# Half tiles of h, split k^T v and a new order of steps in a fused attention and gated convolution kernel

## Chip, cores and metric

The kernel runs on one core of one Trainium2 chip. The metric is the device time of one execution in microseconds; it is quoted as the median of several runs. The core has five engines that run their own instruction queues in order and wait for each other through semaphores: TensorE (PE in the profile, its weight loads PEld), VectorE (DVE), ScalarE (ACT), GpSimd (POOL) and SyncE (SP). PE writes only to PSUM, which has eight banks of 512 fp32 columns; DVE and ACT read it there.

## What is computed

Linear attention without softmax, a normalisation over each head, and a feed-forward layer with a convolution as its gate (8 batches, 8 heads, 576 tokens, head size 64, model 512, inner size 1024):

```python
kv  = einsum('bhsd,bhse->bhde', k, v)
o   = einsum('bhsd,bhde->bhse', q, kv)
x   = o / sqrt(mean(o*o, -1) + 1e-6) * g_norm      # heads side by side: (8, 576, 512)
h   = maximum(x @ w_in, 0)                          # (8, 576, 1024)
c   = conv_w[0]*h[s-1] + conv_w[1]*h[s] + conv_w[2]*h[s+1]
out = (h * sigmoid(c)) @ w_out                      # (8, 576, 512)
```

Inputs and output are fp32; the kernel multiplies in bf16 and accumulates in fp32.

## The kernel before

The order of all work is written out by hand as one long string, `ORDER`. Each word names a step, its arguments and, after `@`, the slots that it takes: a PSUM bank (0 to 7), or a place in a ring of SBUF buffers. The kernel calls the steps in this order, and at the end it ties each engine's instructions to exactly this sequence. So an engine never overtakes a step of its own that waits; what a step waits for follows from the buffers that it reads and takes over.

The steps that matter here, for batch `b`, pair of head tiles `u` (two pairs, `u` = 0, 1), token half `s` (two halves of 288 tokens; batch 0 has 256 and 320) and block `f` of 128 of the 1024 inner columns:

- `pre`, `af`, `ps`, `pl`, `pn`, `pc`, `dg`: the first loads, the identity matrix and small constants. `ps` is twelve small DVE instructions, `pl` nine.
- `cad`, `caa`: casts of batch 0's staged q, k, v to bf16 on DVE or ACT. The other batches are loaded and cast by POOL's DMAs: `Lq`, `Lk`, `Lv`; `Li` loads half of w_in, `Lo` w_out. POOL's queue issues them in their order.
- `qt`, then `qd` or `qa`: q transposed on PE into a bank, copied out by DVE or ACT. `kv.b.u0.n`: k^T v for `n` pairs; `kva`, `kvd`: its copy.
- `ot`: o for one pair and token half. `sq`: its square on ACT. `on` or `oq`: the sum over a head, by a matmul with ones. `nl`: the reciprocal root on ACT. `mo`: x out of o on DVE.
- For batches 4 to 7 the sums of two batches share one bank: `oc` (copy of o), `ss`, `ln`, `sl`, `sp`, `mu` take the place of `on`, `nl`, `mo`.
- `hm.b.f`: one h tile, 8 matmuls of 288 columns into two banks, four for each token half. `re.b.f`: its ReLU on ACT, 576 columns at once. Batch 0 uses `hp` and `rp`, one token half in one bank.
- `ta`, `aa`, `ab` on DVE, `sg` on ACT and `mg` on DVE: taps, sum, sigmoid and gate; `cv`, `sc` do this for four blocks of batch 0 on PE and ACT.
- `om.p.m.f0.n`: half of an output tile of 128 tokens of the batch pair `p`; `ea`, `ed`: its copy by ACT or DVE; `st`: its store by SP. The last tile is `oh`, `eh` or `dh`, `sh`.
- `fi.n.512`: n filler matmuls of zeros, whose result is not used.

In the profile the lines are: L266 `fi`, L382 `kv`, L394 and L396 its copy, L413 `qt`, L440 `ot`, L448 `sq`, L461 and L470 the sums, L478 `nl`, L489 `mo`, L546 `hm`, L552 `re`, L561 `hp`, L568 `rp`, L611 `cv`, L635 `om`, L641 and L646 its copies, L341 `Li`, L327 the loads of q, k, v, L310 and L311 `ps`, L215 ACT's table loads. The reciprocal root and the sigmoid lie in different table sets; the load is issued where the order goes from one to the other.

Of the kernel before, what the change touches and what calls it, by code (L numbers as in the profile page):

```python
# [61 lines left out]
caa.q.1.0 ot.0.0.0@6 sq.0.0.0@0 fi.2.512@1 caa.v.3.0 qt.0.1.0@2 qa.0.1.0@1 oq.0.0.0@4 nl.0.0.0@0 fi.1.512@1 fi.3.512@0  # L62
mo.0.0.0@0 Lk.1.0.4@1 Lv.1.0.4@1 kv.0.1.1@2 fi.1.512@0 Li.4.4 qt.0.0.1@4 Lo.0.8 Lq.2.0.4@2 qd.0.0.1 Lk.2.0.4@0
Lv.2.0.4@0 kva.0.1.1 ot.0.1.0@0 fi.3.512@2 sq.0.1.0@1 oq.0.1.0@6 nl.0.1.0@1 cad.q.1.1 qt.0.1.1@4 qd.0.1.1 ot.0.0.1@2
ot.0.1.1@4 sq.0.0.1@2 sq.0.1.1@3 fi.1.512@6 mo.0.1.0 oq.0.0.1@6 nl.0.0.1@2 fi.1.512@0 fi.1.512@0 mo.0.0.1 oq.0.1.1@0
fi.1.512@6 nl.0.1.1@3 hp.0.0@6 hp.3.0@7 hp.2.0@0 rp.2.0@0 hp.1.0@1 mo.0.1.1 hp.3.1@2 rp.0.0 rp.3.0 pc dg.3 dg.1
hp.1.1@0 rp.1.1 rp.3.1 hp.0.1@3 rp.0.1 dg.0 dg.2 rp.1.0 hp.2.1@4 rp.2.1 qt.1.0.0@6 qd.1.0.0@2 qt.1.1.0@2 qd.1.1.0@3
cv.0.1@0 sc.0.1@0 cv.0.0@4 sc.0.0 mg.0.1.0 cv.0.3@6 sc.0.3@1 cv.0.2@2 sc.0.2 mg.0.1.1 kv.1.0.2@0 kva.1.0.2@1
ot.1.0.1@4 sq.1.0.1@4 ot.1.1.0@6 oq.1.0.1@2 nl.1.0.1@4 mo.1.0.1@1 hp.7.1@0 rp.7.1 hp.6.1@1 rp.6.1 sq.1.1.0@5 hp.7.0@2
rp.7.0 ta.0.1.7@0 Lq.3.0.4@0 Lk.3.0.4@1 Lv.3.0.4@1 Lq.4.0.4@1 hp.6.0@0 rp.6.0 ta.0.1.6 hp.5.0@1 rp.5.0 on.1.1.0@4  # L70
nl.1.1.0@5 mo.1.1.0 ot.1.1.1@2 sq.1.1.1@6 hp.5.1@0 rp.5.1 ta.0.1.5@1 aa.0.1.3 ab.0.1.3 hp.4.1@1 rp.4.1 oq.1.1.1@4
ot.1.0.0@6 nl.1.1.1@6 mo.1.1.1 sq.1.0.0@7 hp.4.0@0 rp.4.0 om.0.0.0.4@1 on.1.0.0@4 nl.1.0.0@7 mo.1.0.0 om.0.3.0.4@0
qt.2.0.0@4 qd.2.0.0@4 qt.2.1.0@2 sg.0.1.7 hm.1.7@6 re.1.7 sg.0.1.6 hm.1.0@4 re.1.0 ta.0.1.4 aa.0.1.2 qd.2.1.0@0
hm.1.1@6 re.1.1 ab.0.1.2 mg.0.1.3 hm.1.2@2 sg.0.1.4 sg.0.1.5 re.1.2 hm.1.3@4 re.1.3 hm.1.4@6 re.1.4 ta.1.1.0@0
ta.1.1.1 aa.1.1.0 ab.1.1.0 sg.1.1.0 sg.1.1.1 kv.2.0.2@2 kvd.2.0.2@2 mg.0.1.2 om.0.1.0.4@4 qt.3.1.0@6 ot.2.0.1@2
sq.2.0.1@0 qd.3.1.0@1 om.0.0.4.4 ed.0.0@0 om.0.3.4.4 ed.0.3@1 ta.1.1.3@1 on.2.0.1@6 om.0.1.4.4 nl.2.0.1@8 mo.2.0.1@2
ed.0.1@2 ot.2.1.1@0 sq.2.1.1@1 ot.2.1.0@6 sq.2.1.0@2 om.0.2.0.4@5 on.2.1.1@2 nl.2.1.1@9 mo.2.1.1 om.0.2.4.4 ea.0.2@3
kv.3.0.2@2 kva.3.0.2@0 on.2.1.0@4 nl.2.1.0@0 mg.1.1.0 mo.2.1.0 ot.2.0.0@0 sq.2.0.0@3 hm.1.6@2 re.1.6 on.2.0.0@4
ta.1.1.2 nl.2.0.0@1 mo.2.0.0 ot.3.1.1@6 sq.3.1.1@4 hm.1.5@2 re.1.5 qt.3.0.0@4 on.3.1.1@0 nl.3.1.1@2 hm.2.5@2 re.2.5@1
# [47 lines left out]
def kernel(  # L127
# [84 lines left out]
    def act_table(which):  # L212
        if act_set[0] != which:
            act_set[0] = which
            nc.scalar.preload_act_table_set(  # L215
                {"rs": "abs_reciprocal_sqrt_and_small", "sig": "sigmoid_and_others"}[which])
# [511 lines left out]
```

## Time and profile before

| | us |
|---|---|
| median of 3 runs | 182.23 (182.22 to 182.25) |
| the profiled execution | 182.22 |
| its span, first to last instruction | 180.1 |
| PE busy | 169.2 |
| ACT busy | 148.8 |
| DVE busy | 148.4 |
| POOL busy | 20.5 |

The span and the busy times come from one profiled execution. The time of an execution is 2.1 us longer than its span. Matmuls are pipelined, so the duration of one in the profile (286 ns for 288 columns) is longer than the distance between two that follow each other; for ACT and DVE too the durations of neighbours overlap a little. The rows that the prediction uses are shown there.

### The profile page before, as it was taken

To read this page: it belongs to the slowest core of one execution; us is meant where nothing else is said; L and a number is where in the kernel's file an instruction comes from. 1 tells how busy PE (TensorE), PEld (TensorE's weight loads), DVE (VectorE), ACT (ScalarE), POOL (GpSimd) and SP (SyncE) were. 2 spreads that over 40 slices of the span, in tenths; PEclk is the share of its full clock that TensorE was granted. 3 is DMA by queue.
4 is the path that set the end of the run, shared out by engine and by line. 5 is a ranking of instruction groups with operands and counts; after the bars stand their busy time and mean duration, and the time that the engine had idled before them with its cause. 6 is when DMAs were issued, how large, how long until landed. Compare 5 with 4: busy or idle time off the path is not lost. (4 is left out here: it accounts for less than half of the span.)

```text
span 180.1 us, 5305 instructions
## 1 busy us (share of the span) xinstructions
PE 169.2 (94%) x2243; PEld 101.5 (56%) x2259; DVE 148.4 (82%) x286; ACT 148.8 (83%) x235; POOL 20.5 (11%) x32
## 2 busy tenths in 40 slices
PE   7878997999999999999999999999999999999991
PEld 2343765577456677546567764445578754444450
DVE  3496853999867899897999999989999899999730
ACT  2377798999888999999989999999699984738830
POOL 3195104000331121030000000000000000000000
PEclk9999999999999999999999999999999999999999
DMA  5999999999999999999440000401160000441495
GB/s 165 393 310 209 208 206 208 208 208 207 208 208 257 208 207 209 207 167 226 143 161 5 0 4 0 151 28 58 64 231 0 0 0 4 175 175 66 175 337 183
DMA packets 20807, 27.80 MB, mean 154 GB/s; under 512 B 1188, under 2 KB 15280, under 8 KB 20784
## 3 DMA queue, kind: packets, MB, share of 16 engines
q0 software_dynamic: 13248, 14.50, 47.7%
q1 hardware_dynamic: 6992, 11.80, 18.2%
q10 hardware_dynamic: 544, 1.18, 1.7%
q8 instruction: 17, 0.28, 0.6%
q14 instruction: 6, 0.05, 0.1%
HBM read 32.52 MB, written 9.44 MB: 233 GB/s over the span
## 5 line engine op out<-in xcount | busy, mean ns | idle before, releaser
L635 PE MATMUL banks<-w_out_sb,h 128*128 128x512 bf16 x267 | 62.8, 379 | 0.9 <-issue 0.5
L546 PE MATMUL banks<-x,w_in_sb 128*128 128x288 bf16 x448 | 58.2, 286 | 0.4 <-ACT rs L478 0.2
L546 PEld LDWEIGHTS <-w_in_sb 128*128 128x128 bf16 x448 | 42.9, 98 | 13.3 <-issue 1.0
L601 ACT ACTIVATE taps<-taps,cw 128x576 bf16<-128x576 bf16 (+1 forms) x44 | 40.6, 958 | 6.5 <-DVE taps L595 6.4
L635 PEld LDWEIGHTS <-h 128*128 128x128 bf16 x280 | 26.3, 98 | 30.5 <-issue 1.5
L552 ACT ACTIVATE h<-banks 128x576 bf16<-128x576 f32 x56 | 34.4, 666 | 2.8 <-PE banks L546 2.2
L625 DVE TENSOR_TENSOR h<-h,taps 128x1152 bf16<-128x1152 bf16 (+1 forms) x24 | 22.8, 953 | 3.6 <-ACT taps L601 1.6
L448 ACT ACTIVATE sq<-banks 128x576 bf16<-128x576 f32 (+2 forms) x32 | 20.9, 686 | 1.8 <-PE banks L440 1.8
L590 DVE TENSOR_TENSOR taps<-taps 128x1152 bf16<-128x1152 bf16 (+1 forms) x22 | 21.5, 977 | 0.5
L595 DVE TENSOR_TENSOR taps<-taps,h 128x1152 bf16<-128x1152 bf16 (+1 forms) x22 | 21.3, 973 | 0.4
L641 ACT ACTIVATE row<-banks 128x512 f32<-128x512 f32 x27 | 15.7, 617 | 4.8 <-PE banks L635 4.1
L584 DVE TENSOR_SCALAR taps<-h,cw 128x576 bf16<-128x576 bf16 (+1 forms) x44 | 18.4, 419 | 1.4 <-ACT h L568 0.7
L489 DVE SCALAR_TENSOR_TENSOR x<-banks,cw,rs 128x576 bf16<-128x576 f32 (+2 forms) x16 | 12.9, 814 | 6.9 <-ACT rs L478 6.8
L585 DVE TENSOR_SCALAR taps<-h,cw 128x576 bf16<-128x576 bf16 (+1 forms) x44 | 18.5, 420 | 0.0
L215 ACT ACT_TABLE_LOAD x10 | 12.8, 1283 | 1.9 <-issue 1.8
L423 DVE COPY qT<-banks 128x1152 bf16<-128x1152 bf16 (+2 forms) x17 | 11.8, 702 | 1.7 <-PE banks L413 1.4
L532 DVE SCALAR_TENSOR_TENSOR x<-o,cw,banks 128x576 bf16<-128x576 f32 x16 | 12.3, 809 | 1.1 <-PE banks L526 1.1
L478 ACT ACTIVATE rs<-banks,eps_sb 128x576 f32<-128x576 f32 (+2 forms) x16 | 11.8, 746 | 1.2 <-PE banks L470 0.5
L266 PE MATMUL banks<-zero 128*128 128x512 bf16 x35 | 10.4, 426 | 1.6 <-DVE zero L245 1.2
L454 ACT ACTIVATE o<-banks 128x576 f32<-128x576 f32 x16 | 10.5, 710 | 0.0
L440 PE MATMUL banks<-qT,kvb 64*64 64x288 bf16 (+2 forms) x128 | 8.5, 297 | 1.4 <-ACT kvb L396 0.9
L327 POOL DMA_DIRECT2D k_sb<-in_k_dram x7 | 5.3, 751 | 38.1 <-PE banks L382 28.2
(80 smaller groups left out, 127.0 us busy)
## 6 DMA issues: line engine op xcount, KB each, us to landing
out_dram<-row SPq DMA_DIRECT2D x35, 256.0 KB, 2.5
q_sb<-in_q_dram POOLq DMA_DIRECT2D x7, 576.0 KB, 16.3
k_sb<-in_k_dram POOLq DMA_DIRECT2D x7, 576.0 KB, 11.6
v_sb<-in_v_dram POOLq DMA_DIRECT2D x7, 576.0 KB, 14.2
stg<-in_v_dram ACTq DMA_DIRECT2D x2, 576.0 KB, 6.4
stg<-in_k_dram SPq DMA_DIRECT2D x4, 288.0 KB, 6.9
w_in_sb<-in_moe_w_in_dram POOLq DMA_DIRECT2D x2, 512.0 KB, 11.2
w_out_sb<-in_moe_w_out_dram POOLq DMA_DIRECT2D x1, 1024.0 KB, 19.4
```

The source lines that it names most:

```text
L448: nc.scalar.activation(T["sq", b, u, s], T["o", b, u, s], AX.Square)
L489: nc.vector.scalar_tensor_tensor(x_part(b, u, s), T["o", b, u, s], g_sb, T["rs", b, u, s], op0=AL.mult, op1=AL.mult)
L546: nc.tensor.matmul(ps[:, s, :c1 - c0], w_in_sb[:, t, f * P:(f + 1) * P], T["x", b][:, t, c0:c1], start=(t == 0), stop=(t == NT - 1))
L552: nc.scalar.activation(h_of(b, f), T["hm", b, f][:, :, :HS].rearrange("p e (r n) -> p e n r", r=R), AX.Relu)
L584: nc.vector.tensor_scalar_mul(tap[:, 0, f % 2, :n, 8:8 + S], h[:, f], cw[:, f:f + 1])
L585: nc.vector.tensor_scalar_mul(tap[:, 1, f % 2, :n, :S], h[:, f], cw[:, 2 * NF + f:2 * NF + f + 1])
L590: nc.vector.tensor_add(tap[:, 1, :, :n, :S], tap[:, 0, :, :n, 7:7 + S], tap[:, 1, :, :n, 1:1 + S])
L595: nc.vector.tensor_add(y, y, span(b, n)[:, 2 * j:2 * j + 2])
L601: nc.scalar.activation(y, y, AX.Sigmoid, scale=cw[:, NF + f:NF + f + 1])
L625: nc.vector.tensor_mul(h, h, tap_of(b, j)[:, 1, :, :n, :S])
L635: nc.tensor.matmul(T["om", p, m], h[:, f, m * P:(m + 1) * P], w_out_sb[:, f, :], start=(f == 0), stop=(f == NF - 1))
L641: nc.scalar.activation(T["os", p, m], T["om", p, m], AX.Copy)
```

## The change

1. The h tiles of batches 1 to 3 are made by token halves: `hs.b.f.s` makes 4 matmuls of 288 columns into one bank, `rh.b.f.s` does the ReLU of 288 columns. 24 `hm` and 24 `re` become 48 `hs` and 48 `rh`. Batches 4 to 7 keep `hm` and `re`.
2. `kv.1.0.2` becomes `kv.1.0.1` and `kv.1.1.1`, with a copy each (one on ACT, one on DVE).
3. POOL's queue gets the second half of w_in in front of q, k and v of batch 1; before it stood behind them.
4. The whole `ORDER` is new: other places for nearly all steps and banks, 44 filler matmuls where there were 38, eight output copies fewer or more on one or the other engine (ACT's 27 become 23, DVE's 8 become 12, and of the two short ones at the end DVE takes one). ACT runs 253 instructions where it ran 235, DVE 293 where it ran 286.

Steps that no word of `ORDER` calls (`tq`, `kz`, `kx`, `ox`, `sv`) are added too, and with them the names `TQ`, `GW` and `width`. As no word calls `tq`, `TQ` is empty, `GW` is `HS` as before, and all widths are as they were.

```diff
 ORDER = """
-pre@0,1 pl fi.10.512@0 af cad.q.0.0@0 caa.v.0.0@0 caa.k.0.0@0 qt.0.0.0@2 gt.k.1.0 cad.v.1.0 Li.0.4 Lq.1.0.4@1
-fi.13.512@0 qd.0.0.0@0 cad.k.1.0 ct@0 kv.0.0.1@4 kva.0.0.1@0 ps cad.v.2.0 pg cad.k.2.0 cad.k.3.0 cad.q.0.1 fi.1.512@1
...
-cv.0.1@0 sc.0.1@0 cv.0.0@4 sc.0.0 mg.0.1.0 cv.0.3@6 sc.0.3@1 cv.0.2@2 sc.0.2 mg.0.1.1 kv.1.0.2@0 kva.1.0.2@1
-ot.1.0.1@4 sq.1.0.1@4 ot.1.1.0@6 oq.1.0.1@2 nl.1.0.1@4 mo.1.0.1@1 hp.7.1@0 rp.7.1 hp.6.1@1 rp.6.1 sq.1.1.0@5 hp.7.0@2
...
-hm.1.1@6 re.1.1 ab.0.1.2 mg.0.1.3 hm.1.2@2 sg.0.1.4 sg.0.1.5 re.1.2 hm.1.3@4 re.1.3 hm.1.4@6 re.1.4 ta.1.1.0@0
...
+pre@0,1 fi.10.512@0 af ps gt.k.1.0 Li.0.4 cad.q.0.0@0 qt.0.0.0@2 caa.v.0.0@0 pn fi.8.512@0 ct@0 fi.5.512@1 cad.v.1.0
+pg cad.k.1.0@0 caa.k.0.0 kv.0.0.1@4 fi.2.512@0 kva.0.0.1@0 qd.0.0.0@0 ot.0.0.0@6 fi.2.512@0 cad.q.1.0 qt.0.1.0@2
...
+qt.0.1.1@2 qd.0.1.1 ot.0.0.1@0 sq.0.0.1@2 mo.0.1.0 ot.0.1.1@2 sq.0.1.1@3 fi.1.512@6 oq.0.0.1@6 nl.0.0.1@2 pl mo.0.0.1
+fi.1.512@4 oq.0.1.1@4 nl.0.1.1@3 mo.0.1.1 hp.2.0@6 hp.0.0@7 rp.0.0@0 hp.3.0@4 rp.2.0 pc dg.2 dg.0 dg.3 Li.4.4
+Lq.1.0.4@1 Lk.1.0.4@1 dg.1 hp.1.0@5 rp.1.0 hp.2.1@7 hp.0.1@6 rp.0.1 rp.3.0 hp.1.1@5 rp.1.1 hp.7.0@0 rp.7.0 rp.2.1
...
+ab.0.1.3 cv.0.3@6 sc.0.3@0 cv.0.2@2 sc.0.2 mg.0.1.1 hp.5.1@4 rp.5.1 kv.1.0.1@6 kva.1.0.1@1 hp.5.0@5 rp.5.0 ot.1.0.0@0
+sq.1.0.0@4 ot.1.0.1@2 kv.1.1.1@6 sq.1.0.1@5 kvd.1.1.1 ta.0.1.4@0 ta.0.1.5 aa.0.1.2 fi.1.512@4 fi.1.512@4 oq.1.0.0@4
+nl.1.0.0@4 mo.1.0.0@1 fi.6.512@6 oq.1.0.1@6 nl.1.0.1@5 mo.1.0.1 ot.1.1.1@4 sq.1.1.1@6 ot.1.1.0@6 sq.1.1.0@7 oq.1.1.1@0
+ab.0.1.2 nl.1.1.1@6 mo.1.1.1 om.0.0.0.4@2 on.1.1.0@0 nl.1.1.0@7 mo.1.1.0 om.0.1.0.4@3 hs.1.3.1@4 Lq.2.0.4@2 qt.2.1.0@0
+qd.2.1.0@4 qt.2.0.0@6 hs.1.0.1@5 qd.2.0.0@0 sg.0.1.5 sg.0.1.4 hs.1.1.1@0 rh.1.1.1 mg.0.1.2 hs.1.1.0@1 rh.1.1.0
...
+om.0.6.4.4 ed.0.6@0 ss.4.4.2@7 ss.5.4.2 ln.4@0 sl.4@0 qt.6.0.0@4 qd.6.0.0@1 qt.6.1.0@0 qa.6.1.0@4 hs.3.7.1@2 rh.3.7.1
+hs.3.4.0@3 rh.3.4.0 hs.3.6.1@7 rh.3.6.1 hs.2.4.1@6 st.0.8 rh.2.4.1 hs.3.6.0@0 rh.3.6.0 hs.3.5.1@1 rh.3.5.1
+sp.4.1.0.4@2 mu.4.1.0@1 sp.4.1.1.4@6 hs.2.7.1@0 rh.2.7.1 mu.4.1.1 hs.3.4.1@1 rh.3.4.1 sp.4.0.0.4@4 mu.4.0.0
+sp.4.0.1.4@2 mu.4.0.1 sg.2.2.3 hs.3.5.0@0 hs.3.7.0@1 rh.3.5.0 sp.5.1.0.4@6 mu.5.1.0@0 kv.6.0.2@4 kvd.6.0.2@0
+hs.2.6.0@2 rh.2.6.0 sp.5.0.1.4@6 mu.5.0.1 hm.4.5@4 sp.5.1.1.4@2 rh.3.7.0 sp.5.0.0.4@0 mu.5.0.0 mu.5.1.1 sg.2.2.0
...
 """
...
+    @op
+    def hs(b, f, s):
+        c0, c1 = cols(b, s)
+        ps = T["hs", b, f, s] = bank()[:, :c1 - c0]
+        for t in range(NT):
+            nc.tensor.matmul(
+                ps, w_in_sb[:, t, f * P:(f + 1) * P], T["x", b][:, t, c0:c1],
+                start=(t == 0), stop=(t == NT - 1))
+
+    @op
+    def rh(b, f, s):
+        ps, h = T["hs", b, f, s], h_of(b, f)
+        if b in TQ:
+            h, fr = h.rearrange("p (n r) -> p n r", r=R)[:, :, s::2], ps.rearrange("p (g n) -> p n g", n=PS)
+        else:
+            h = h[:, s * HS:(s + 1) * HS].rearrange("p (n r) -> p n r", r=R)
+            fr = ps.rearrange("p (r n) -> p n r", r=R)
+        nc.scalar.activation(h, fr, AX.Relu)
```

More of the change, by code (lines that the diff above doesn't have):

```diff
@@ L75 @@
[L75 to L79, printed above, removed]
@@ L123 @@
+ea.3.4@0 st.3.4 oh.3.8.0@3 dh.3.8.0@5 sh.3.8.0 oh.3.8.1@2 eh.3.8.1@4 sh.3.8.1
 """
@@ L216, in act_table @@
                 {"rs": "abs_reciprocal_sqrt_and_small", "sig": "sigmoid_and_others"}[which])
+    TQ = {int(tok.split("@")[0].split(".")[1]) for tok in ORDER.split() if tok.startswith("tq.")}
     RS = ((0, 4), (4, 9))
+    GW = 320 if TQ else HS
     HEAD = (("sync", "q.0.0 k.0.1 k.1.1 q.1.0 k.2.1 k.3.1 q.0.1 q.1.1"), ("scalar", "v.0.2 v.2.2"))
@@ L223, in cols, with width @@
             return tuple(r * D for r in RS[s])
+        if b in TQ:
+            return s * 5 * D, (5 + s * 4) * D
         return s * HS, (s + 1) * HS
+    def width(b, s):
+        c0, c1 = cols(b, s)
+        return c1 - c0
     @op
@@ L444, in sq, with tq, kz, kx @@
     @op
+    def tq(b, u):
+        T["qT", b, u] = ring("qT", [P, 2, S], BF16, "qT").rearrange("p a s -> p (a s)")
+        nc.sync.dma_start_transpose(
+            out=T["qT", b, u].rearrange("p (g c) -> p g c", c=P),
+            in_=qkv["q", b][:, 2 * u:2 * u + 2, :].rearrange("p t c -> p (t c)"))
+    @op
+    def kz(b, u0, n):
+        k_sb, v_sb = qkv["k", b], qkv["v", b]
+        ps = T["kv", b, u0] = bank2()
+        for u in range(u0, u0 + n):
+            for r in range(R):
+                for tt in range(2):
+                    for i in range(2):
+                        nc.tensor.matmul(
+                            ps[half(tt), i, u * D:(u + 1) * D],
+                            k_sb[half(i), 2 * u + tt, r * D:(r + 1) * D],
+                            v_sb[half(i), 2 * u + tt, r * D:(r + 1) * D],
+                            start=(r == 0), stop=(r == R - 1))
+    @op
+    def kx(b):
+        T["kvx", b] = ring("kvx", [P, 2, 2 * D], BF16, "kvx")
+        for i in range(2):
+            nc.sync.dma_start(out=T["kvx", b][half(i)], in_=T["kvb", b][half(1 - i)])
+    @op
+    def ox(b, u, s):
+        ps = T["o", b, u, s] = bank2()[:, :, :width(b, s)]
+        qt_sb = T["qT", b, u].rearrange("p (g i c) -> p g i c", i=2, c=D)
+        kv_sb = T["kvx" if s else "kvb", b]
+        for tt in range(2):
+            c = half(tt ^ s)
+            g0 = (tt * R + s) // 2
+            for i in range(2):
+                nc.tensor.matmul(
+                    ps[half(i), tt, :].rearrange("p (g c) -> p g c", c=D),
+                    kv_sb[c, i, u * D:(u + 1) * D], qt_sb[c, g0:g0 + 5 - s, i, :],
+                    start=True, stop=True)
+    @op
     def sq(b, u, s):
@@ L448, in sq, with sv @@
         nc.scalar.activation(T["sq", b, u, s], T["o", b, u, s], AX.Square)
+    @op
+    def sv(b, u, s):
+        c0, c1 = cols(b, s)
+        T["sq", b, u, s] = ring("sq", [P, 2, 320], BF16, "sq")[:, :, :c1 - c0]
+        nc.vector.tensor_mul(T["sq", b, u, s], T["o", b, u, s], T["o", b, u, s])
     @op
@@ L494, in ss @@
         if b == b0:
-            T["ss", b0] = bank()[:, :HS]
+            T["ss", b0] = bank()[:, :GW]
         for s in range(2):
@@ L504, in ln @@
     def ln(b0):
-        r = T["rs", b0] = ring("rs", [P, HS], FP32, "rs")
+        r = T["rs", b0] = ring("rs", [P, GW], FP32, "rs")
         act_table("rs")
@@ L511, in sl @@
         r = T["rs", b0]
-        w = T["w", b0] = ring("w", [P, HS], BF16, "wparts")
-        hi = work.tile([P, HS], BF16, name="hi", bufs=1)
+        w = T["w", b0] = ring("w", [P, GW], BF16, "wparts")
+        hi = work.tile([P, GW], BF16, name="hi", bufs=1)
         nc.vector.tensor_copy(hi, r)
@@ L520, in sp @@
     def sp(b, u, s, b0):
-        ps = T["sp", b, u, s] = bank2()[:, :, :HS]
+        ps = T["sp", b, u, s] = bank2()[:, :, :width(b, s)]
         c = 2 * (b - b0) + s
@@ L526, in sp @@
             nc.tensor.matmul(
-                ps[:, tt, :], spread[rows, 2 * c:2 * c + 2, :].rearrange("p i d -> p (i d)"), T["w", b0][rows, :],
+                ps[:, tt, :], spread[rows, 2 * c:2 * c + 2, :].rearrange("p i d -> p (i d)"), T["w", b0][rows, :width(b, s)],
                 start=True, stop=True)
@@ L544, in hm @@
             for s in range(2):
-                c0, c1 = cols(b, s)
+                c0, c1 = s * HS, (s + 1) * HS
                 nc.tensor.matmul(
-                    ps[:, s, :c1 - c0], w_in_sb[:, t, f * P:(f + 1) * P], T["x", b][:, t, c0:c1],
+                    ps[:, s, :HS], w_in_sb[:, t, f * P:(f + 1) * P], T["x", b][:, t, c0:c1],
                     start=(t == 0), stop=(t == NT - 1))
```

112 lines of the change are left out of this document (58 added, 54 removed).

## The prediction

> **What bounds the kernel now.** I read the page first, then a table of windows by stage, the chain that ended last, the groups by line and shape, and the timeline of each engine. The page and the table (columns: stretch, its length, then busy time and count for PE, PEld, DVE, ACT, POOL, granted clock, DMA share, GB/s):
>
> ```profile
> span 180.1 us, 5305 instructions
> PE 169.2 (94%) x2243; PEld 101.5 (56%) x2259; DVE 148.4 (82%) x286; ACT 148.8 (83%) x235; POOL 20.5 (11%) x32
> ...
> 18.02:37.51 19.49, 17.72 (x341) 12.40 (x341) 13.31 (x34) 17.52 (x33) 2.96 (x4) 1.00 1.22 207
> 37.51:50.00 12.49, 12.38 (x190) 7.91 (x193) 11.48 (x22) 11.70 (x18) 2.23 (x3) 1.00 1.21 208
> 50.00:66.00 16.00, 15.50 (x354) 10.16 (x352) 12.48 (x22) 14.60 (x24) 3.71 (x5) 1.00 1.20 222
> 66.00:83.00 17.00, 16.79 (x333) 10.39 (x337) 16.14 (x27) 17.00 (x32) 2.23 (x3) 1.00 1.17 196
> 83.00:107.00 24.00, 23.72 (x400) 16.63 (x400) 22.55 (x37) 23.21 (x34) 0.00 (x0) 1.00 0.29 85
> 130.00:174.00 44.00, 43.84 (x255) 25.07 (x256) 40.58 (x73) 32.83 (x50) 0.00 (x0) 1.00 0.31 114
> ```
>
> PE is idle for 0.1 to 0.5 us in each stage from 37.5 on, at full clock. So PE's own work sets the end, and whatever PE loses anywhere is never won back. ACT is just as full from 66 to 107 (17.00 of 17.00, then 23.21 of 24.00); DVE has 3.4 us free in the last row. The chain of waits says the same of the end:
>
> ```profile
> 128.23 16.66 PE banks L546 x136
> ...
> 145.16 10.74 PE banks L635 x49
> ...
> 173.46 0.61 ACT row L641
> 174.07 0.02 issue
> 174.09 1.98 DMA out_dram<-row
> ```
>
> These rows also give PE's prices back to back: 16.66/136 = 0.1225 us for a matmul of 288 columns, 10.74/49 = 0.219 us for one of 512. The profiled execution took 182.22 us, 2.1 us of them outside the span; the median is 182.23, so the sum is made on 182.2. A difference under 0.2% (0.36 us) can't be told from none.
>
> **PE's work does not change.** Eight matmuls of 288 columns make one h tile of batches 1 to 3, as one block (hm) or as two halves (hs); the weight is loaded for each matmul either way. That one bank takes four accumulations in a row costs nothing: batch 0's h already runs that way (L561, 256 or 320 columns):
>
> ```profile
> 18.02 4.08 PE L561 MATMUL banks<-x,w_in_sb 128*128 128x256 bf16 x32
> 22.03 0.80 PE L413 MATMUL banks<-ident,q_sb 64*64 64x64 bf16 x72
> 25.83 0.78 PE L382 MATMUL banks<-v_sb,k_sb 64*64 64x64 bf16 x72
> 27.12 0.44 PE L440 MATMUL banks<-qT,kvb 64*64 64x288 bf16 x8 [0.52 <-ACT kvb L396]
> ```
>
> 16 matmuls of 256 and 16 of 320 columns took 22.03 - 18.02 = 4.01 us, 0.50 per half tile, 0.435 ns a column against 0.1225/288 = 0.425. The k^T v of batch 1 keeps its 72 matmuls. Fillers rise from 38 to 44. They fill waits and make none, so I count the waits, not them.
>
> **The head, up to the first matmul of h: -0.25.** The `ps` step moves from behind the cast of k.1 to the front of DVE's queue:
>
> ```profile
> 4.94 0.43 DVE L364 CAST q_sb<-stq 128x512 bf16<-128x512 f32 x1 [1.88 <-DMA stq<-in_q_dram]
> ...
> 8.90 1.94 DVE L310 TENSOR_TENSOR bg<-bg,ident 128x8 bf16<-128x8 bf16 x10
> 10.87 0.45 DVE L311 COPY spread<-bg 128x512 bf16<-128x512 bf16 x1
> 11.25 0.44 DVE L364 CAST v_sb<-stg 128x576 bf16<-128x576 f32 x1
> ```
>
> It lasts 2.6 us (8.71 to 11.32). Started as soon as the identity stands, near 3.1, it ends near 5.7, so the first cast of q slips by 0.7 us, and with it qt, kv, ot of the first block, all queued behind it. In return the casts of v and k for the second block no longer wait for it. DVE, ACT and PE alternate afterwards as before, and `pl` (about 1.0 us of memsets) now stands between two scalings. Following the block's steps by their rows, the last two normalisations come 0.25 us earlier than in
>
> ```profile
> 16.96 1.72 ACT L478 ACTIVATE rs<-banks,eps_sb 128x640 f32<-128x640 f32 x2
> ```
>
> and the first h half, which takes over bank 6 from the first of them, starts at 17.8 instead of 18.02. Bounds: -0.9 (the whole of what stood behind `ps`, less the slip) to +0.7 (the slip alone).
>
> **w_in in front of batch 1: 0, and it lengthens a bare chain: +0.7.** POOL's queue now issues both halves of w_in, then q, k, v of batch 1, then w_out. In all as many bytes stand ahead of w_out, so v of batch 1 lands when the second half of w_in did:
>
> ```profile
> 11.98 0.93 POOL L341 DMA_DIRECT2D w_in_sb<-in_moe_w_in_dram  x1
> ...
> DMA to landing us min/median/max: 7.3/11.2/15.1
> ```
>
> 11.98 + 15.1 = 27.1 us. PE needs it after 15 halves of h, four convolutions and two transposes: 17.8 + 15 x 0.49 + (25.83 - 22.03) = 28.9. It is there, with 1.8 us to spare.
>
> But before, batch 1's attention was woven between the h halves of blocks 4 to 7; afterwards all but one of these are done when it starts. What is left is a chain through ACT:
>
> ```profile
> L396 ACT ACTIVATE kvb<-banks 128x128 bf16<-128x128 f32 x2 | 0.6, 277 | 2.9 <-PE banks L382 2.9
> ...
> 46.48 1.28 ACT L215 ACT_TABLE_LOAD   x1
> 47.87 0.74 ACT L478 ACTIVATE rs<-banks,eps_sb 128x576 f32<-128x576 f32 x1
> 49.00 1.19 ACT L448 ACTIVATE sq<-banks 128x576 bf16<-128x576 f32 x2 [0.38 <-PE banks L440]
> ...
> 62.57 1.37 ACT L478 ACTIVATE rs<-banks,eps_sb 128x576 f32<-128x576 f32 x2
> ```
>
> One piece of k^T v 0.35 + 0.06; its copy 0.28 + 0.05; o up to its square 0.37; two squares at 1.19 - 0.65 = 0.54 apart; table load 1.28; two normalisations 0.64 apart; two squares; the third normalisation 0.74: 0.74 + 0.37 + 1.08 + 1.28 + 1.28 + 1.08 + 0.74 = 6.6 us. One more sum of squares and half a block of the output (4 x 0.219) stand ahead of the first h half of batch 1: 6.6 + 0.3 + 0.9 = 7.8 us. PE's work in it: k^T v 0.7, one h half 0.44, o and sums of squares about 1.4, two half blocks of output 1.75: 4.3. So 3.5 us are lost (eight fillers, 1.7 us, lie in them), and about 0.5 before it where PE changes between 64- and 128-wide tiles: 4.0. The same sum for before: h 16 x 0.49, 3.80 for transposes and convolutions, 0.7, 1.4, 1.75, two transposes 0.73 = 16.2 of the 19.49 us of its row, 3.3 lost. Difference +0.7; splitting k^T v is in it, its second piece hides behind the squares. Bounds: -0.5 (the 0.5 us and half of the chain's lags fall away) to +1.8 (each lag of 0.2 comes to 0.3).
>
> **h in halves: +1.0 on ACT's side.** The prices of a ReLU out of a bank, alone and back to back:
>
> ```profile
> L552 ACT ACTIVATE h<-banks 128x576 bf16<-128x576 f32 x56 | 34.4, 666 | 2.8 <-PE banks L546 2.2
> L568 ACT ACTIVATE h<-banks 128x320 bf16<-128x320 f32 x8 | 3.4, 497 | 0.3 <-PE banks L561 0.3
> L568 ACT ACTIVATE h<-banks 128x256 bf16<-128x256 f32 x8 | 3.1, 477 | 1.0 <-PE banks L561 1.0
> ...
> 19.65 1.06 ACT L568 ACTIVATE h<-banks 128x256 bf16<-128x256 f32 x3 [0.97 <-PE banks L561]
> 21.05 1.80 ACT L568 ACTIVATE h<-banks 128x320 bf16<-128x320 f32 x5 [0.34 <-PE banks L561]
> ...
> 68.46 2.79 ACT L552 ACTIVATE h<-banks 128x576 bf16<-128x576 f32 x5
> L641 ACT ACTIVATE row<-banks 128x512 f32<-128x512 f32 x27 | 15.7, 617 | 4.8 <-PE banks L635 4.1
> ```
>
> Back to back: whole (2.79 - 0.66)/4 = 0.53; 256 wide (1.06 - 0.48)/2 = 0.29; 320 wide (1.80 - 0.50)/4 = 0.325; so 288 wide 0.31, a pair 0.62. Alone: 2 x 0.487 against 0.666. 24 pairs add 24 x 0.09 = 2.0 us, or 24 x 0.31 = 7.4. Against it four output copies of 0.617, and half a dozen smaller ones, move to DVE; the table loads stay at ten. Packed, ACT's total is unchanged. The Trainium skill, ScalarE: Activation LUTs, "Rules for kernel authors", budgets about 0.3 us for each ACTIVATE and 0.83 ns an element: an estimate from that page is 0.54 for a half and 0.78 for a whole, 7.2 us for 24 pairs, and a sum of about 187. The rows agree with it for one standing alone and not for one in a queue.
>
> What decides is where they fall. By the order, eleven halves (5.5 tiles) still stand behind batch 4's first normalisation, where before four whole tiles did. A half is made in 0.49 us by PE and read in 0.31: ACT idles 0.18 in each, 2.0 in eleven, in the stretch (83 to 107) in which it had 0.8 us free. About 1.2 comes through to PE's wait for banks. In 50 to 66 banks come free a little sooner (PE idles 0.5 there): -0.2. Bounds for both: -0.5 to +4.0 (7.4, less the copies that moved and ACT's 0.8 and 1.4 us free).
>
> **Late stages: 0.** DVE gets four more copies of 0.69 and a short one, about 3 us, most of them before 84 or after the last gate, and it had 3.4 us free. The last evacuation still starts right behind the last matmul. If the cover is gone: +2.
>
> **Sum.** 182.2 - 0.25 + 0.7 + 1.0 = 183.65, say 183.7.
>
> **Rivals.** Faster: the half banks repay. PE idles 1.8 us in 18 to 37.5 and 0.5 in 50 to 66; if a half freed 0.2 us sooner is what PE waits for, and the attention of batch 1 closes up by the 0.5 of its bound, the sum is 182.2 - 0.25 - 0.5 - 0.4 = 181.1. It decides as soon as PE's lost time up to the first h of batch 1 is below 3.3 us. For it: w_in is there early, and PE can run 11 us without a wait. Against it: the chain's rows, a table load and three normalisations one behind the other, with 4.3 us of PE's work beside 7.8. Much slower: each half pays as if alone, 7.4 less 3 for the copies that moved: 186.6; against it, the rows of five and three in a queue. No change: the bounds' middle, -0.25 + 0.7 - 0.5: 182.2. That the change does not do what it says is left out: the order names each half.
>
> **Chances.** Forecast 0.55, with 182.7 to 185 of its own; faster 0.27; none 0.08; much slower 0.10. Range 181.3 to 185.5: it leaves out the far end of the two outer cases. Faster by over 0.2%: 0.27, within: 0.08, slower: 0.65.
>
> **What would show it.** The first h matmul at 17.8; the first of batch 1 near 17.8 + 15.5 + 4.0 = 37.3, with the two transposes of batch 2 (0.73) still to come, where before they were done at 37.51; ReLUs of halves near 0.49; batch 4's first normalisation no earlier than 85; PE idle over 1 us between 83 and 107. It is wrong if PE loses less than 3.3 us before batch 1's h, or ACT has gaps after 84 while PE has none.

## The result, and the profile after

The changed kernel takes 185.34 us (median of 4 runs, 185.17 to 185.92), the kernel before 182.24 in the same session: ratio 1.0174 (95% interval 1.0151 to 1.0198). The direction was forecast, the size was not: +3.1 us against +1.5. Medians are over all executions of a run; the ratios leave out an execution that is over 1.5% above the fastest of its kernel.

The page of the changed kernel, and the table by stage with the stretches that were shown of before (the last row is new):

```profile
span 183.0 us, 5338 instructions
PE 171.5 (94%) x2250; PEld 102.2 (56%) x2265; DVE 153.0 (84%) x293; ACT 148.0 (81%) x253; POOL 20.7 (11%) x32
...
18.02:37.51 19.49, 18.50 (x279) 12.48 (x278) 14.83 (x38) 16.84 (x33) 2.96 (x4) 1.00 1.22 208
37.51:50.00 12.49, 12.28 (x250) 7.56 (x250) 10.08 (x18) 11.55 (x20) 2.23 (x3) 1.00 1.21 209
50.00:66.00 16.00, 15.87 (x337) 11.50 (x335) 13.74 (x25) 15.41 (x33) 2.24 (x3) 1.00 1.20 220
66.00:83.00 17.00, 16.84 (x302) 9.28 (x303) 16.47 (x27) 16.80 (x36) 4.02 (x5) 1.00 1.02 167
83.00:107.00 24.00, 22.47 (x318) 15.86 (x316) 21.20 (x31) 22.15 (x36) 0.00 (x0) 1.00 0.36 82
130.00:174.00 44.00, 43.84 (x261) 25.57 (x263) 42.41 (x76) 32.46 (x51) 0.00 (x0) 1.00 0.25 94
174.00:184.00 10.00, 3.61 (x25) 2.23 (x23) 1.11 (x2) 1.97 (x4) 0.00 (x0) 0.79 0.61 222
```

From 37.5 on only one stage has a hole in PE: 83 to 107, 1.53 us of 24. From 50 to 66 PE is fuller than before (15.87 against 15.50). And the span is 2.9 us longer while PE finishes only 1.6 us later: 175.70 + 1.91 against 174.08 + 1.93, by the last group of matmuls in the two timelines.

```profile
174.08 1.93 PE L660 MATMUL banks<-w_out_sb,h 128*128 128x256 bf16 x16
```

```profile
175.70 1.91 PE L739 MATMUL banks<-w_out_sb,h 128*128 128x256 bf16 x16
```

So 1.3 us arise behind PE, which the prediction had put at nothing. The mean granted clock of 0.991 is no loss: it is 1.00 in every stretch up to 174 and falls once PE has stopped.

Busy time hides short waits, because a matmul that waits in the pipeline counts as busy. A sharper measure is PE's lost time: the point in time at which PE loads the weights of a step, less PE's own work ahead of it at the back-to-back prices. These are 0.1225 us for 288 columns, 0.216 for 512 and 0.0102 for one of the 64x64 matmuls of the transposes and of k^T v (72 of them, two transposes in a row, take 0.73 us); the few other narrow ones are priced in the same way, and fillers count as loss. It was counted over all weight loads of each trace. The first column stands at the first load for h, the others at the first load behind that much own work; since the steps differ, a difference between two rows is good to about 0.1 us:

| us of own work done | first h (3) | 20 | 46 | 62 | 68 | 100 | end |
|---|---|---|---|---|---|---|---|
| before | 14.81 | 18.21 | 21.35 | 22.38 | 22.97 | 24.94 | 25.07 |
| after | 14.54 | 18.90 | 20.95 | 22.25 | 24.45 | 26.57 | 26.67 |
| after, seventh row buffer | 14.56 | 18.92 | 20.97 | 22.28 | 22.87 | 25.02 | 25.13 |
| after, both repairs (second run) | 14.21 | 18.57 | 20.61 | 21.91 | 22.51 | 24.63 | 24.73 |
| before, h in halves only | 14.94 | 18.34 | 21.30 | 22.79 | 23.57 | 25.53 | 25.67 |
| after, both repairs, old head | 14.85 | 18.25 | 21.73 | 23.04 | 23.64 | 25.81 | 25.91 |

At 20 us of work batch 1's attention is over in all of them. After less before, from column to column: -0.3 up to the first h, +1.0 in batch 1's attention, -0.8 from there to 62 us of work, then +1.6 within 6 us of work, and 0.1 behind it. At 62 the new order had won back what it lost in batch 1's attention and was 0.1 us ahead of the old one; then it lost 1.6 us in one place.

**The place.** The timeline of the changed kernel there:

```profile
79.13 0.68 DVE L725 COPY row<-banks 128x512 f32<-128x512 f32 x1
...
79.83 1.83 SPq L730 DMA_DIRECT2D out_dram<-row  x4
...
83.54 0.68 DVE L725 COPY row<-banks 128x512 f32<-128x512 f32 x1
...
84.08 0.50 ACT L567 ACTIVATE rs<-banks,eps_sb 128x288 f32<-128x288 f32 x1
...
85.49 1.01 ACT L633 ACTIVATE h<-banks 128x288 bf16<-128x288 f32 x3
85.99 0.69 DVE L725 COPY row<-banks 128x512 f32<-128x512 f32 x1 [1.78 <-ACT h L633]
...
86.73 1.63 PE L621 MATMUL banks<-x,w_in_sb 128*128 128x288 bf16 x12 [1.33 <-DVE row L725]
```

PE waits 1.33 us for a bank that DVE empties into a row buffer, and DVE has been idle for 1.78 us in front of that copy. The profile names ACT's ReLU as the releaser, but the copy (`ed.0.6@0`) reads nothing of that ReLU. It writes row buffer 0, which `ed.0.4@0` filled at 79.13 and the store issued at 79.83 has to read first. The view of that tile has the time from issue to landing, here of the stores between 70 and 100 us in the changed kernel:

```profile
L730 SPq DMA_DIRECT2D out_dram<-row x4: 332/427/444, 79.8 to 81.2; - x4
...
DMA to landing us min/median/max: 6.0/8.7/10.2
```

79.83 + 6.0 = 85.9, just ahead of the copy at 85.99. The last loads of q, k and v share the DMA engines with it (share 1.02 from 66 to 83). In the kernel before, the stores of the same window are six with 2.1/2.8/7.3.

**The tail.** DVE now copies rows 0, 2 and 3 of the last pair behind its last gating product; before, ACT copied 0 and 3 earlier.

```profile
171.36 0.76 DVE L704 TENSOR_TENSOR h<-h,taps 128x1152 bf16<-128x1152 bf16 x1 [0.65 <-ACT taps L680]
172.03 1.88 DVE L725 COPY row<-banks 128x512 f32<-128x512 f32 x3
...
173.31 1.09 ACT L720 ACTIVATE row<-banks 128x512 f32<-128x512 f32 x2 [1.98 <-PE banks L714]
174.91 0.60 ACT L720 ACTIVATE row<-banks 128x512 f32<-128x512 f32 x1 [0.51 <-DMA out_dram<-row]
...
176.06 0.60 ACT L720 ACTIVATE row<-banks 128x512 f32<-128x512 f32 x1 [0.56 <-DMA out_dram<-row]
177.15 0.42 DVE L754 COPY row<-banks 128x256 f32<-128x256 f32 x1 [1.43 <-PE banks L739]
177.70 0.38 ACT L749 ACTIVATE row<-banks 128x256 f32<-128x256 f32 x1 [1.04 <-PE banks L739]
177.80 1.32 SPq L759 DMA_DIRECT2D out_dram<-row  x2
```

The last copy still starts right behind the last matmul (177.70), as predicted. But the stores bunch up behind it, and the table by single microseconds shows the DMA engines full until 180 and busy for half of the microsecond behind it:

```profile
178.00:179.00 1.00, 0.00 (x0) 0.00 (x0) 0.00 (x0) 0.08 (x1) 0.00 (x0) 1.00 1.05 381
179.00:180.00 1.00, 0.00 (x0) 0.00 (x0) 0.00 (x0) 0.00 (x0) 0.00 (x0) 0.88 1.00 352
180.00:181.00 1.00, 0.00 (x0) 0.00 (x0) 0.00 (x0) 0.00 (x0) 0.00 (x0) 0.50 0.42 144
```

In the kernel before the same view has a share of 0.95 from 177 to 178 and 0.01 behind it.

### The profile page after: what moved, and what is told of

Same layout as the page of the kernel before. It is cut to its first block, busy times and chain, and to the rows that moved or that the text cites. A ratio compares the mean times of both kernels' runs of the same rounds, so it can differ in the third digit from the quotient of the medians.

```text
span 183.0 us, 5338 instructions
## 1 busy us (share of the span) xinstructions
PE 171.5 (94%) x2250; PEld 102.2 (56%) x2265; DVE 153.0 (84%) x293; ACT 148.0 (81%) x253; POOL 20.7 (11%) x32
## 4 chain that ended last, share of the span: by engine, by line
PE 75%; DVE 7%; ACT 7%; issue 4%; DMA 3%; POOL 1%; DVEq 0%; POOLq 0%; ACTq 0%
PE banks L714 30%; PE banks L606 14%; PE banks L621 10%; PE banks L640 4%; DMA out_dram<-row 3%; PE banks L426 3%; PE banks L279 3%; PE banks L395 3%; PE banks L453 2%; PE banks L690 2%; ACT taps L680 2%; ACT sq L502 1%; ACT rs L538 1%; ACT h L612 1%; PE banks L521 1%
## 5 line engine op out<-in xcount | busy, mean ns | idle before, releaser
L606 PE MATMUL banks<-x,w_in_sb 128*128 128x288 bf16 x256 | 32.5, 286 | 0.1
L621 PE MATMUL banks<-x,w_in_sb 128*128 128x288 bf16 x192 | 27.6, 286 | 1.3 <-DVE row L725 1.3
L502 ACT ACTIVATE sq<-banks 128x576 bf16<-128x576 f32 (+2 forms) x32 | 20.4, 672 | 1.6 <-PE banks L453 1.6
L612 ACT ACTIVATE h<-banks 128x576 bf16<-128x576 f32 x32 | 19.2, 686 | 1.6 <-PE banks L606 1.6
L633 ACT ACTIVATE h<-banks 128x288 bf16<-128x288 f32 x48 | 18.1, 417 | 1.9 <-PE banks L621 1.6
L664 DVE TENSOR_SCALAR taps<-h,cw 128x576 bf16<-128x576 bf16 (+1 forms) x44 | 19.4, 441 | 0.0
L663 DVE TENSOR_SCALAR taps<-h,cw 128x576 bf16<-128x576 bf16 (+1 forms) x44 | 18.7, 425 | 0.7 <-ACT h L633 0.5
L720 ACT ACTIVATE row<-banks 128x512 f32<-128x512 f32 x23 | 13.1, 601 | 3.9 <-PE banks L714 2.8
L279 PE MATMUL banks<-zero 128*128 128x512 bf16 x41 | 13.0, 443 | 1.7 <-DVE zero L258 1.2
L436 DVE COPY qT<-banks 128x1152 bf16<-128x1152 bf16 (+2 forms) x16 | 10.8, 693 | 1.8 <-PE banks L426 1.8
```

The lines of the kernel that those rows point to most:

```text
L279: nc.tensor.matmul(ps[:, :w], zero[:, :P], zero[:, :w], start=True, stop=True)
L502: nc.scalar.activation(T["sq", b, u, s], T["o", b, u, s], AX.Square)
L606: nc.tensor.matmul(ps[:, s, :HS], w_in_sb[:, t, f * P:(f + 1) * P], T["x", b][:, t, c0:c1], start=(t == 0), stop=(t == NT - 1))
L612: nc.scalar.activation(h_of(b, f), T["hm", b, f][:, :, :HS].rearrange("p e (r n) -> p e n r", r=R), AX.Relu)
L621: nc.tensor.matmul(ps, w_in_sb[:, t, f * P:(f + 1) * P], T["x", b][:, t, c0:c1], start=(t == 0), stop=(t == NT - 1))
L663: nc.vector.tensor_scalar_mul(tap[:, 0, f % 2, :n, 8:8 + S], h[:, f], cw[:, f:f + 1])
```

## The experiments

All ratios are to the kernel before on the same chip, with 95% intervals. Line numbers in the experiments are one or two lower than in the changed kernel.

### A seventh row buffer

```diff
-ed.0.6@0
+ed.0.6@6
```

> The changed kernel, with the copy of row tile 6 of the first pair of batches put into a seventh row buffer instead of the one that row tile 4 left (its store landed at 85.87 us). Theory A (the row buffer): DVE waited 1.78 us for that store, hs.2.4.1 waited for bank 6 behind DVE, so PE lost 1.5 us at 85 to 87; with a buffer free, the copy starts near 84.2, the PE wait falls to under 0.3 us and the kernel takes 183.8 to 184.2 us (185.3 less 1.2 to 1.5). Theory B (ACT and the half banks bound this stretch, as predicted): the wait moves to the next halves, and the kernel takes 185.0 to 185.4 us.

183.44 us, ratio 1.0051 (1.0034 to 1.0068): 1.9 us less than the changed kernel. The same place in its timeline:

```profile
83.56 1.28 DVE L724 COPY row<-banks 128x512 f32<-128x512 f32 x2
83.74 2.86 PEld L620 LDWEIGHTS <-w_in_sb 128*128 128x128 bf16 x24
83.74 3.16 PE L620 MATMUL banks<-x,w_in_sb 128*128 128x288 bf16 x24
```

The two copies run back to back, 24 matmuls of h run without a gap, and the lost time from 62 to 68 falls from 2.20 to 0.60, which is what the kernel before has there. Theory A is shown, and B falls: nothing on ACT takes the wait's place (PE is busy for 23.89 of the 24.00 us from 83 to 107). The gain in the time is 0.3 us over that in the two traces, whose spans differ by 1.55 us (183.0 and 181.4); the other executions of this run have spans of 181.1 to 181.3, and those of the changed kernel 183.0 to 183.1.

### The last rows copied earlier

```diff
-ed.3.0@1 ... ed.3.2@5 ... ed.3.3@0
+om.3.0.4.4 ea.3.0@6 sg.7.1.6 st.2.6 st.3.0 ea.2.2@1
+om.3.3.4.4 ea.3.2@5 ea.3.3@0 st.3.2 st.3.3
```

> The changed kernel, with the copies of rows 0, 2 and 3 of the last pair of batches on ACT, in gaps that it has before 172 us, instead of on DVE behind its last gating product, and their stores moved up. Theory A (the tail): PE ends 1.6 us later than in the kernel before, but the last store lands 3.15 us later, since eight rows were stored in one burst from 173.9 on; spread out, the last store lands 2.0 to 2.4 us after the last copy instead of 3.5, and the kernel takes 184.0 to 184.4 us. Theory B (the tail only follows PE): 185.2 to 185.5 us.

183.21 us, ratio 1.0037 (1.0023 to 1.0050): 2.1 us less than the changed kernel, more than expected. Theory A holds: in the trace of this run the last store lands 2.35 us behind PE's last matmul, where it landed 3.97 us behind it in the changed kernel. Another 0.4 us lies in the closing of the execution behind that landing (1.0 us against 1.4). Two old stores that were still queued late (rows 7 of the first pair and 2 of the second) stayed late here, so they were not the cause.

The profiled execution of this run took 186.13 us, the five others 182.83 to 183.32. Its trace shows the wait for the row buffer, which this run does not mend, at its worst: the store of row tile 4 took 8.0 us to land, where it took 5.9 to 6.2 in six other traces with the stores in the same order.

```profile
87.60 0.69 DVE L724 COPY row<-banks 128x512 f32<-128x512 f32 x1 [3.70 <-DMA out_dram<-row]
...
88.35 2.08 PE L620 MATMUL banks<-x,w_in_sb 128*128 128x288 bf16 x8 [3.25 <-DVE row L724]
```

### Both repairs

> Both edits of the two runs above together. If the row buffer and the burst of stores are separate causes, the gains add: 182.4 to 182.9 us, that is the kernel before plus at most 0.7 us. If one only uncovers the other or ACT: 183.5 us or more.

181.51 us, ratio 0.9951 (0.9935 to 0.9967). A second run on another occasion, with five rounds:

> The run with both repairs once more, on the same chip as the one beside it, to fix its distance from the kernel before: 181.4 to 181.9 us, ratio 0.993 to 0.997.

181.35 us, ratio 0.9948 (0.9935 to 0.9960). The gains add, and a little more: the changed kernel with two local repairs is 0.9 us faster than the kernel before. The table of the second run at the two places:

```profile
83.00:107.00 24.00, 23.84 (x428) 17.16 (x417) 22.79 (x33) 23.43 (x39) 0.00 (x0) 1.00 0.34 79
...
177.00:178.00 1.00, 0.00 (x0) 0.00 (x0) 0.00 (x0) 0.00 (x0) 0.00 (x0) 1.00 0.56 188
178.00:179.00 1.00, 0.00 (x0) 0.00 (x0) 0.00 (x0) 0.00 (x0) 0.00 (x0) 1.00 0.03 8
```

Where the 0.9 us lie is settled only in part. From the first h to the end PE loses 10.52 us (24.73 - 14.21) against 10.26 before, so the order itself costs 0.3. The first h comes at a lost time of 14.40 us on the average of ten traces with the new head and 14.82 of four with the old one: -0.4, and -0.6 in this pair of traces. Another 0.5 us is saved in the closing after the last store, 1.1 us in both traces here and 1.6 in the kernel before; what shortens it is not shown.

### The halves alone

```diff
-hm.1.7@6 re.1.7
+hs.1.7.0@6 hs.1.7.1@7 rh.1.7.0 rh.1.7.1
```

and so for all 24 tiles of batches 1 to 3, in the order of the kernel before.

> The kernel before in its own order, with each h tile of batches 1 to 3 made as two halves one behind the other in the two banks that the whole tile took, and read by two ReLUs. Only the halving is left of the change. The prediction's step (24 more ReLUs at 0.09 us when packed, ACT full from 66 to 107): +1.0 to +2.0 us, 183.2 to 184.2 us. Rival, the half banks repay (PE lost 1.25 us less from 37 to 66 us in the changed kernel): 181.4 to 182.2 us. Each half as if alone: 186 us or more.

182.99 us, ratio 1.0031 (1.0020 to 1.0042): +0.65 us, under the prediction's +1.0 to +2.0 and far under the price of halves that stand alone. The groups by line, the ReLUs of the kernel before and then of this one:

```profile
L552 ACT ACTIVATE h<-banks 128x576 bf16<-128x576 f32 x56 | 34.4, 666 | 2.8 <-PE banks L546 2.2
```

```profile
L610 ACT ACTIVATE h<-banks 128x576 bf16<-128x576 f32 x32 | 19.6, 677 | 1.9 <-PE banks L604 1.8
L631 ACT ACTIVATE h<-banks 128x288 bf16<-128x288 f32 x48 | 16.5, 436 | 0.1
```

19.6 + 16.5 - 34.4 = 1.7 us more on ACT for 24 pairs; the prediction had 2.0 packed, and ACT waits 0.1 us in front of all 48. About 0.5 us of it reaches PE, between 46 and 68 us of work (0.60 at the end of the table, less the 0.13 that this trace has more already at the first h). The rival falls too: in the old order halves repay nothing. So what the changed kernel gains from 20 to 62 us of work is put down to the order, with halves in it; no run has the new order with whole tiles.

### The old head in the new order, the new head in the old

> The changed kernel with both repairs (row buffer, last rows), and with the head and the attention of batch 1 as the kernel before has them: second half of w_in behind batch 1, k^T v of batch 1 in one piece, its attention woven between the h halves of blocks 4 to 7; from the first h half of batch 1 on, the changed order. In the two traces PE had lost 18.57 us at batch 1's h in the changed kernel and 17.78 before. Theory A (that loss is never won back): 0.8 us less than the run with both repairs, 180.5 to 180.9 us. Theory B (a stage behind it is bound by ACT or by loads and takes the time back): 181.3 us or more.

> The kernel before, with the changed head and attention of batch 1 (w_in whole in front of it, k^T v in two pieces, its chain bare) up to the first h of batch 1, then the old order with whole tiles. The prediction's terms: -0.25 for the head, +0.7 for the chain: 182.7 us. By the lost time in the traces, -0.3 and +1.1: 183.0 to 183.2 us. If later stages take it back: 182.3 us.

185.29 us, ratio 1.0175 (1.0158 to 1.0192), and 187.34 us, ratio 1.0266 (1.0231 to 1.0301). Both say nothing on the head: in each, the joint of the two orders made waits of its own. In the first, an output block came into a bank that batch 1's scaling still held (2.1 us), in the second, k^T v stood behind a tap buffer (2.1 us). The second order also writes the convolution of block 3 (`sc.0.3`) into the tap buffer in which the sums of batch 0's blocks 6 and 7 still wait for their gate, so these are overwritten, and its time is not that of the same computation. Again with these two mended:

> The changed kernel with both repairs, and with the head and the attention of batch 1 as the kernel before has them; this time the first output row block stays in bank 1 (banks 0 and 3, and 1 and 2, change places from there on), so that it does not wait for batch 1's scalings on DVE, and the gating of blocks 6 and 7 comes ahead of that of 4 and 5 as before. The earlier run of this idea lost 2.1 us at that bank and 1.85 us behind batch 2's first transposes, which the joint and not the change made. Theory A (what PE loses in batch 1's chain is never won back): 0.8 us less than the run with both repairs, 180.5 to 180.9 us, if the joint adds no wait. Theory B (a later stage takes it back): 181.3 us or more with no new wait at the joint.

> The kernel before, with the changed head and attention of batch 1 up to its first h, the tap buffers left as the change has them (the earlier run of this idea made k^T v wait 2.2 us for a tap buffer). The prediction's terms: -0.25 for the head, +0.7 for the chain: 182.7 us. By the lost time in the traces, -0.3 and +1.1: 183.0 to 183.2 us. If later stages take it back: 182.3 us.

The old head in the new order: 182.45 us, ratio 1.0009 (0.9999 to 1.0018), 0.9 to 1.1 us slower than with the new head, where 0.8 faster was expected. Between the first h and 20 us of work it loses 3.39 us, as the kernel before does (3.40), against 4.36: the chain's price is there. From there to 46 us of work it loses 3.49, and the kernel with the new head 2.04. (The 0.8 us of the expectation were read at batch 1's first h, where the two kernels had not done the same work; at 20 us of work the two traces are 0.7 apart.) The table from 37.5 to 66, of the new head and then of the old:

```profile
37.50:66.00 28.50, 28.16 (x583) 19.26 (x585) 23.82 (x42) 26.97 (x54) 4.45 (x6) 1.00 1.20 215
```

```profile
37.50:66.00 28.50, 27.45 (x572) 18.14 (x557) 24.61 (x49) 25.62 (x52) 4.47 (x6) 1.00 1.20 215
```

In the changed kernel DVE makes the taps and sums of batch 0's blocks 4 and 5 while PE waits in batch 1's chain (31.12 to 35.92 us); with the old head all of these but the taps of block 5 stand behind it (39.17 to 41.39 us), at the start of batch 2's work. So the two parts seem to belong together: PE's wait in the chain buys DVE a lead which the next stage uses. That the lead is the cause of the 1.45 us, or of all of it, is not shown, since this joint too moved steps.

The new head in the old order: 184.87 us, ratio 1.0137 (1.0101 to 1.0173). It loses 6.7 us between the first h and 20 us of work, 2.3 more than the same head in its own order, so the joint still waits and the price can't be read from it. Part of it is the granted clock, which reads 0.68 and 0.50 in the two stretches from 36 to 40 us of this trace; two of the four executions took 185.4 us with a mean clock of 0.991, as the traced one, the others 184.2 and 184.3 with 0.997. Behind 20 us of work it loses 6.9 us, just like the kernel before (6.9): there nothing was given back.

### k^T v of batch 1 in one piece

```diff
-kv.1.0.1@6 kva.1.0.1@1 ... kv.1.1.1@6 ... kvd.1.1.1
+kv.1.0.2@6 kva.1.0.2@1
```

> The changed kernel with both repairs, but k^T v of batch 1 in one piece of 72 matmuls at the place of the first piece. The prediction put the split at nothing beyond the chain: its first piece lets the chain through ACT start 0.35 us earlier, its second hides behind the squares. If so, this kernel is 0.3 to 0.4 us slower than the run with both repairs beside it; if the chain's start does not matter, equal; if two pieces cost more than one (two more changes of tile form), up to 0.3 us faster.

181.71 us, ratio 0.9979 (0.9961 to 0.9998), against 0.9948 for both repairs beside it: 0.36 us slower, as the prediction's chain says. In the traces it loses 4.66 us between the first h and 20 us of work, against 4.36. The split is worth its two instructions.

### The store later, and the hole filled

```diff
-st.0.0 st.0.4 ... st.0.5 st.0.2
+st.0.0 ... st.0.5 st.0.2 st.0.4
```

> The changed kernel without repairs, with the store of row tile 4 of the first pair issued behind two other stores, so that its row buffer comes free later. Theory A (PE at 85 us waits for that store): the landing moves from 85.9 to about 90 us, PE's hole from 1.5 to 5 us or more, and the kernel takes 188.5 us or more; if the granted clock falls behind so long a hole, up to 191. Theory B (another wait bounds that place): 185.3 us.

> The same as the run with the later store, with 18 matmuls of zeros (18 x 0.216 = 3.9 us) into a free bank in front of the waiting h half. They do no work, and the store lands no sooner. If the granted clock falls in the hole and stays low behind it, this kernel is faster than the one with the hole by that part (1 to 2 us); if only the wait counts, the two are equal.

186.09 us (184.79 and 187.39) and 188.09 us (187.79 and 188.39), two executions each, so the first can't be told from the changed kernel (185.34). Both expectations missed: with the other two stores out of the way early, the store in question was issued at the old time and landed only 1 us later in the traced execution (187.39). Now the profile names the releaser, in the timeline of the first:

```profile
87.04 0.69 DVE L724 COPY row<-banks 128x512 f32<-128x512 f32 x1 [3.17 <-DMA out_dram<-row]
...
87.79 2.49 PE L620 MATMUL banks<-x,w_in_sb 128*128 128x288 bf16 x10 [2.71 <-DVE row L724]
```

and behind a hole of 2.71 us the granted clock (third column from the right) falls, in its table:

```profile
85.00:87.00 2.00, 0.07 (x1) 0.00 (x0) 0.00 (x0) 1.16 (x4) 0.00 (x0) 1.00 1.16 248
87.00:89.00 2.00, 1.21 (x6) 0.83 (x6) 1.85 (x5) 0.13 (x1) 0.00 (x0) 0.72 1.20 208
89.00:91.00 2.00, 2.00 (x12) 0.91 (x10) 1.07 (x2) 0.90 (x3) 0.00 (x0) 0.50 0.57 99
91.00:93.00 2.00, 2.00 (x19) 1.05 (x16) 1.82 (x3) 1.12 (x4) 0.00 (x0) 0.92 0.00 0
```

The hole in the unrepaired kernel, 1.33 us, left it at 1.00. With the hole filled the clock stayed at 1.00 throughout, but 18 fillers were too many: they ran to 89.3, while the copy had been free at 86.2. That copy would have ended the hole after some 1.5 us, not much more than the 1.33 us that left the clock at 1.00. So the run shows neither that fillers hold the clock nor whether a fitting number would pay.

## Why the prediction was right or wrong

**Head: right.** First matmul of h predicted at 17.8, found at 17.78 (before 18.02). Over all traces the first h's lost time is 14.18 to 14.76 us with the new head and 14.67 to 14.94 with the old one, so one pair of traces can miss the gain by its own size.

```profile
17.78 1.47 PE L640 MATMUL banks<-x,w_in_sb 128*128 128x256 bf16 x12 [0.18 <-ACT rs L538]
```

**Batch 1's chain: right, a little small, and not lost for good.** w_in did not make k^T v wait, and batch 1's first h stands at 37.28 (predicted 37.3), both transposes of batch 2 behind it. Lost from the first h to 20 us of work: 4.36 against 3.40, +1.0 where +0.7 was said, inside its bounds. The rival that closes the attention up (under 3.3 us lost) falls. But the premise that whatever PE loses is never won back is borne out in the old order only, where the new head got nothing back; by 62 us of work the new order had made this loss good, and with the old head it was not faster.

```profile
37.28 0.65 PE L621 MATMUL banks<-x,w_in_sb 128*128 128x288 bf16 x4
```

**h in halves: too large for the halves, and the new order left out.** The step "+1.0" took ACT's extra time (24 x 0.09 is 2.2, not the 2.0 that it said) and let 1.2 us of it through between 83 and 107. Halving alone costs +0.65 us, but in the order in which it was done PE loses 6.20 us from 20 us of work to the end (with the row buffer repaired) against 6.86 before: -0.7. The step priced the halves in the old order's stages and gave the new order 0.2 us. ACT's count held: 148.0 us in all against 148.8, and 0.30 us from half to half in a queue (the three in 1.01 us at 85.49; one took 0.417 on the average of all 48, where 0.49 was said):

```profile
L633 ACT ACTIVATE h<-banks 128x288 bf16<-128x288 f32 x48 | 18.1, 417 | 1.9 <-PE banks L621 1.6
```

The sign set for it failed too: batch 4's first normalisation came at 84.08, not after 85. The estimate of 7.2 us for 24 pairs does not agree with the 1.7 us measured. The Trainium skill, ScalarE: Activation LUTs, "Rules for kernel authors", states its 0.3 us for an ACTIVATE with the bias as a pointer operand. These ReLUs have no such operand, and in a queue they come closer together than one of them takes (0.30 us against 0.417), so the rule was not one for this case.

**PE idle over 1 us between 83 and 107: right, for a wrong reason.** It was 1.53 us, of which ACT made none that shows: with a seventh row buffer 0.11 us are left. The failed step is the list of what a copy waits for: the prediction followed banks, engines and loads, and no row buffer and no store. That is 1.6 us of PE's lost time in the trace and 1.9 in the time.

**Late stages: 0, wrong.** The 3.4 us that DVE had free were there (1.6 of them are left from 130 to 174), and the last evacuation still starts right behind the last matmul, and both are beside the point. Slack in a stage says nothing on when in it a copy can run: in DVE's order the copies stood behind its last gating. The alternative "+2 if the cover is gone" came true, with +1.3 in the trace.

The sum with the measured terms: -0.3 + 1.0 - 0.7 + 1.6 + 1.3 = 2.9, the difference of the spans. The first three, which the prediction had, come to 0.0 where it said +1.45; the two that it did not see or priced at nothing are the result. So that the kernel came out slower, as forecast, and inside the stated range was luck: without the two local waits it is 0.9 us faster than the kernel before.

## What to carry to other kernels

When a copy out of a bank moves to another engine or another place, follow its destination as well as its source: which buffer it writes, which store must have landed first, and how long stores take while loads share the DMA engines. Price the last stores by when the last few rows become ready, not by the last copy alone. And do not judge a new order by its time alone: here two local waits cost more than all the rest of the change moved, and without them it was the faster kernel.

## What the hardware showed that was not expected

- A store of 256 KB lands 2.0 us after its issue at the quickest (the view of the row tile from 164 us on, below), and 6.0 to 10.2 us after it beside the loads. The Trainium skill, DMA: Bandwidth & Descriptors, "Anatomy of one DMA — SWDGE (gpsimd) path", gives a fixed 2.0 us and the bytes at 436 GB/s for one transfer, 2.6 us as an estimate for this one, though SP issues it here: above the quickest and near the median at the end, far from the stores beside loads.

```profile
L730 SPq DMA_DIRECT2D out_dram<-row x17: 332/433/983, 165.1 to 177.1; - x17
...
DMA to landing us min/median/max: 2.0/2.9/3.9
```

- A hole of 1.3 us on PE left the granted clock at 1.00, one of 2.7 us was followed by a clock of 0.72, 0.50 and 0.92 over the next 6 us, and one of 3.25 us (the trace of the last rows copied earlier) by 0.98, 0.50 and 0.67 from 86 to 92. Each of these adds up to 3.4 us at half clock, by (0.28 + 0.50 + 0.08) x 2 / 0.5 for the first. The length of one hole does not decide it: of the first two joint runs, each with a hole of 2.07 us, the clock stayed at 1.00 in one and read 0.89, 0.50 and 0.75 from 31 to 37 us in the other, and in the mended new head in the old order it fell with no hole over 0.83 us, behind a stretch of 2 us in which PE was busy for 0.75. The Trainium skill, TensorE: Matmul & The Clock Gate, "Part 1: The HAM clock gate", has half rate after an idle window of about 3.4 us that runs freely. The level agrees; the holes here were shorter than the window that it states.
- An idle time's named releaser can be an instruction that the waiting one does not depend on: the same copy was put down to a ReLU in one trace and to the store in another.
